# A decode kernel: fewer, larger VectorE instructions per K tile, and w2 in two halves with a cast and a store each

## The chip, the cores and the metric

The kernel runs on one core of one Trainium2 chip. The metric is the device time of one execution in microseconds (us). The kernel before takes 661.6 us, and its own runs lie within 0.7 us of each other in any one set of rounds. The span in a profile is about 1.5 us shorter than the timed run. A load "lands" when the last of its 16 parts, one for each DMA engine, has reported its end. The profile also records the TensorE clock as 1.0 (full) or 0.5 (half).

## The reference, cut to what matters

Four sequences decode one token. An attention block over a cache of 4096 positions and 32 heads is followed by a small dense block. The caches dominate: `k_cache` and `v_cache` are 134 MB each, all weights together 15 MB.

```python
q = (layernorm(x) @ wq)                        # 4 x 640 -> 4 x 32 x 128
scores = einsum("bhqd,bhkd->bhqk", q, k_cache) * Dh ** -0.5
o = einsum("bhqk,bhkd->bhqd", softmax(scores), v_cache)
h = x + o.reshape(B, Sq, H * Dh) @ wo
act = mish(layernorm(h) @ w1 + b1)
out = h + act @ w2                             # w2: 1728 x 640
```

## The kernel before

The caches are cut into 16 K tiles and 16 V tiles of 8.4 MB (8 heads of one sequence each). They pass through three SBUF slots, A, B and C. All loads are issued by one engine, SyncE, in order, into one queue. Tiles come in four groups of four (`b` is 0 to 3). The order of loads and what each waits for:

```python
for hg in range(NHG):                       # i = hg * 4 is the group's first tile
    ...
    sp.need(("F", i + 1, NS - 1)); k_load(i + 3)      # slot B
    sp.need(("F", i + 2, NS - 1)); v_load(i + 2)      # slot A: free when the last fold of K tile i+2 is done
    sp.need(("PV", i + 1));        v_load(i + 3)      # slot C
```

For each K tile, in four slices `s`: VectorE multiplies the slice with q in place (`M`), TensorE adds up columns by 16 matmuls with an identity (`F`, the "fold"), VectorE reduces the rest (`R`), ScalarE takes exp. When the four slices are through, VectorE spreads the exp values over 8 head columns (the mask, `e`) and TensorE multiplies with V (`PV`). The VectorE order of a tile, and TensorE's order for the third and fourth tile of a group:

```python
# VectorE, tile i
mult(i, 0); mult(i, 1); reduce(i, 0); mult(i, 2)
reduce(i, 1); mult(i, 3); reduce(i, 2); reduce(i, 3)
for s in range(NS):
    mask(i, s)
# TensorE
for b in (2, 3):
    fold(i + b, 0); fold(i + b, 1); fold(i + b, 2)
    pv_mm(i + b - 1)
    fold(i + b, 3)
    o_mm(i + b - 1)
```

At the end the weights come through the same queue: wo, w1, and w2 last, in pieces. The 640 output columns are computed as four groups of 160 on four column groups of TensorE, cast by one VectorE instruction, and stored by two DMAs on each of two queues. Four dummy matmuls (`busy(4)`) stand before the w2 matmuls, while TensorE waits for `act`.

The softmax here doesn't subtract the row's maximum and nothing guards it: scores larger than these inputs give would overflow.

Of the kernel before, what the change touches and what calls it, by code (L numbers as in the profile page):

```python
# [7 lines left out]
FP32 = mybir.dt.float32  # L8
# [70 lines left out]
def kernel(  # L79
# [39 lines left out]
    OC = D // CG  # L119
# [39 lines left out]
    rs1 = sb("rs1", (P, N), FP32)  # L159
    rsm = sb("rsm", (P, N, G), FP32)  # L160
    rl = sb("rl", (BG, 1), FP32)
    bmask = sb("bmask", (BG, G), FP32)
    rlm = sb("rlm", (BG, G), FP32)
    hmask_f = sb("hmask_f", (P, G), FP32)
    hmask = sb("hmask", (P, G), BF16)
    delta_f = sb("delta_f", (BG, N), FP32)
# [30 lines left out]
    zeros = sb("zeros", (P, OC), BF16, tail, topA)  # L197
# [3 lines left out]
    mu = sb("mu", (P, N), FP32, tail, topA)  # L201
    esq = sb("esq", (P, N), FP32, tail, topA)
    cen = sb("cen", (P, DC, N), BF16, tail, topA)
    msq = sb("msq", (P, N), FP32, tail, topA)
# [6 lines left out]
    h_hi = sb("h_hi", (P, DC, N), BF16, tail, topA)  # L211
    h_lo = sb("h_lo", (P, DC, N), BF16, tail, topA)
# [27 lines left out]
    y2_ps = red[:, 0, 0:OC]  # L240
# [24 lines left out]
    def store(p, h):  # L265
        p.need("o_bf")
        for k in range(h, CG, 2):
            load(
                p, out_rows[:, k * OC : (k + 1) * OC], o_bf[k * QD : k * QD + N, :],
                ("out", k), f"OUT{h}",  # L270
            )

    def leave(p, h):
        fin, o = book.handles["FIN"], book.handles[f"OUT{h}"]
        if p.live:
            p.eng.sem_inc(fin, 1)
            p.eng.wait_ge(o, 32).then_inc(o, -32)
# [73 lines left out]
    def pool_prog():  # L351
# [13 lines left out]
        po.do(lambda: g.memset(ones[:, :], 1.0), "ones", "PO")  # L365
        po.need(("PV", NT - 2))
        po.do(lambda: g.memset(ones_d[:, :], 1.0 / D), "ones_d", "PO")
        po.do(lambda: g.memset(zeros[:, :], 0.0), "zeros", "PO")

    def act_prog():  # L370
# [21 lines left out]

        ac.need("ident")
# [7 lines left out]
        def exp(i, s):  # L401
# [8 lines left out]
                ("exp", i, s), "AC",  # L410
# [31 lines left out]
        )  # L442
        store(ac, 1)
        leave(ac, 1)

    def dve_prog():
# [5 lines left out]
        for k in range(2):  # L452
# [14 lines left out]
                out=hmask_f[:, :], in_=ident[:, :].rearrange("p (g q) -> p g q", g=G),  # L467
                axis=AX.X, op=ALU.add,
            ),
            "hmask_f", DV,  # L470
# [3 lines left out]
                out=bmask[:, :], in_=ident[0:BG, 0:BG].rearrange("p (b g) -> p g b", g=G),  # L474
                axis=AX.X, op=ALU.add,
            ),
            "bmask", DV,
        )
        dv.do(
            lambda: v.tensor_reduce(  # L480
                out=delta_f[:, :], in_=ident[0:BG, 0:BG].rearrange("p (b g) -> p b g", g=G),
                axis=AX.X, op=ALU.add,
            ),
            "delta_f", DV,
# [10 lines left out]
        dv.need("delta_f")  # L495
        dv.do(lambda: v.tensor_copy(out=hmask[:, :], in_=hmask_f[:, :]), "hmask", DV)
        dv.do(lambda: v.tensor_copy(out=delta[:, :], in_=delta_f[:, :]), "delta", DVP)
# [20 lines left out]
        dv.need("b1p", "b1z")  # L518
        dv.do(lambda: v.tensor_copy(out=b1T[:, 0:FM], in_=b1_ps[:, 0:FM]), "b1m", DV)  # L519
        dv.do(lambda: v.tensor_copy(out=b1T[0:FT, FM:FC], in_=b1_ps[0:FT, FM:FC]), "b1T", DVP)  # L520
        dv.do(lambda: v.memset(rsm[:, :, :], 1.0), ("rsm", -1), DVP)
        dv.need(("qc", N - 1), "hmask")

        def mult(i, s):
            hg, b = divmod(i, N)
            t = slot[KS[b]][:, :].rearrange("p (r d) -> p r d", d=Dh)[:, s * RS : (s + 1) * RS, :]
            dv.need(("K", i))
            dv.do(
                lambda: v.tensor_tensor(  # L529
                    out=t, in0=t, in1=q_bc[:, hg, b, :].unsqueeze(1).to_broadcast([P, RS, Dh]),  # L530
                    op=ALU.mult,
                ),
                ("M", i, s), DVP,
            )
# [13 lines left out]
        def mask(i, s):  # L548
            sl = slice(s * RS, (s + 1) * RS)
            dv.need(("exp", i, s))  # L550
            if i:
# [3 lines left out]
                    out=e[:, sl, :], in0=ex[:, sl].unsqueeze(2).to_broadcast([P, RS, G]),  # L555
                    in1=hmask[:, :].unsqueeze(1).to_broadcast([P, RS, G]), op=ALU.mult,
                ),
                ("e", i, s), DVP,
            )

        def sums(hg):
            dv.do(
                lambda: v.tensor_reduce(
                    out=rs1[:, :], in_=rs[:, :, :], axis=AX.X, op=ALU.add
                ),
                ("rs1", hg), DV,
            )
            dv.need(("rs1", hg))
            dv.do(
                lambda: v.tensor_tensor(  # L570
                    out=rsm[:, :, :], in0=rs1[:, :].unsqueeze(2).to_broadcast([P, N, G]),
                    in1=hmask[:, :].unsqueeze(1).to_broadcast([P, N, G]), op=ALU.mult,
# [4 lines left out]
        def norm(hg):  # L577
            dv.need(("L", hg))
            dv.do(lambda: v.reciprocal(out=rl[:, :], in_=l_ps), ("rl", hg), DV)  # L579
            dv.need(("rl", hg))  # L580
            dv.do(
                lambda: v.tensor_scalar(
                    out=rlm[:, :], in0=bmask[:, :], scalar1=rl[:, :], scalar2=None, op0=ALU.mult
                ),
                ("rlm", hg), DV,
            )
            dv.need(("rlm", hg), ("O", hg * N + N - 1))
            dv.do(
                lambda: v.tensor_tensor(
                    out=om[:, :, :], in0=o_ps.unsqueeze(1).to_broadcast([BG, G, Dh]),  # L590
                    in1=rlm[:, :].unsqueeze(2).to_broadcast([BG, G, Dh]), op=ALU.mult,
# [10 lines left out]
        for i in range(NT):  # L602
            hg, b = divmod(i, N)
            mult(i, 0)
            mult(i, 1)
            reduce(i, 0)
# [430 lines left out]
```

## Time and profile before

Median 661.67 us (661.51 to 661.71, 3 runs). Profiled span 660.0 us.

| what | value | where |
|---|---|---|
| share of 16 DMA engines' span in the load queue | 99.4% | the DMA queues |
| spacing of 8.4 MB tiles at the end of the queue | 19.3 us each | landing records |
| VectorE busy | 62% | the busy table |
| slack of the third V load of each group over the end of the load ahead of it | 9.3, 6.8, 7.7, 9.0 us | issue times and landing records |
| from the last landing to the end | 2.5 us | 660.04 - 657.57 |

The page of the kernel before: its span, the busy times by engine, the DMA rate in 40 equal slices, the load queue (packets, MB, share of 16 engines), and two instruction groups with count, busy time, mean ns of one, and the idle time ahead of them. PE is TensorE, DVE VectorE, ACT ScalarE; SPq is SyncE issuing a DMA, PEq TensorE's instruction sequencer; L529 is line 529 of the kernel.

```profile
span 660.0 us, 4989 instructions
...
PE 383.8 (58%) x2636; PEld 68.4 (10%) x1680; DVE 407.8 (62%) x257; ACT 40.7 (6%) x157; POOL 1.7 (0%) x12
...
GB/s 418 409 445 445 438 441 417 422 441 438 438 437 425 429 437 437 441 437 421 433 437 437 441 437 417 437 437 433 441 441 417 437 433 437 441 441 417 425 416 312
...
q1 hardware_dynamic: 6912, 283.35, 99.4%
...
L529 DVE TENSOR_TENSOR slotA<-slotA,q_bc 128x8192 bf16<-128x8192 bf16 x32 | 140.7, 4416 | 93.1 <-DMA slotA<-in_A_k_cache_dram 93.1
...
L554 DVE TENSOR_TENSOR e<-ex,hmask 128x512 bf16<-128x512 bf16 x64 | 39.8, 684 | 0.0
```

The DMA row never falls below 409 GB/s before the last slice: the kernel runs at the rate of its loads. Work on the engines costs time only where a load is issued too late, or after the last load has landed.

The timeline of the kernel before around the third K tile of the second group (start us, length us, engine, what; in brackets the idle time before it):

```profile
250.67 8.75 DVE L529 TENSOR_TENSOR slotA<-slotA,q_bc 128x8192 bf16<-128x8192 bf16 x2
255.24 0.59 PE L730 MATMUL red<-slotA,ident 128*128 128x512 bf16 x1 [8.15 <-PEq L49]
255.62 5.99 PE L740 MATMUL red<-slotA,ident 128*128 128x512 bf16 x15
261.64 1.23 DVE L540 TENSOR_REDUCE s_f<-red 128x64 f32<-128x1024 f32 x1 [2.21 <-PE red L740]
262.78 4.42 DVE L529 TENSOR_TENSOR slotA<-slotA,q_bc 128x8192 bf16<-128x8192 bf16 x1
...
267.34 0.38 PE L730 MATMUL red<-slotA,ident 128*128 128x512 bf16 x1 [2.29 <-PEq L49]
267.56 5.08 PE L740 MATMUL red<-slotA,ident 128*128 128x512 bf16 x15
...
272.57 3.64 PE L730 MATMUL pv<-slotC,e 128*32 128x512 bf16 x64
...
276.37 3.40 PE L740 MATMUL red<-slotA,ident 128*128 128x512 bf16 x15
...
279.80 0.33 SPq L263 DMA_DIRECT2D slotA<-in_A_v_cache_dram  x1
```

The four folds start at 255.2, 261.4, 267.3 and 276.1. The last one releases the V load at 279.80. The load ahead of it landed at 286.61, so it was issued 6.8 us ahead of need.

The end of the kernel before, from the same view:

```profile
652.03 0.71 PE L730 MATMUL red<-cen,slotB 128*64 128x4 bf16 x14
...
652.78 0.22 DVE L693 TENSOR_TENSOR h<-red,rstd 128x56 f32<-128x56 f32 x1 [2.85 <-PE red L730]
...
654.32 0.22 DVE L719 SCALAR_TENSOR_TENSOR act<-tb,hm 128x56 bf16<-128x56 f32 x1
...
655.13 1.27 PE L730 MATMUL red<-slotA,act 128*4 128x160 bf16 x32
...
657.23 0.62 PE L730 MATMUL red<-slotA,act 128*4 128x160 bf16 x20 [0.83 <-DMA slotA<-in_B_w_dram]
657.91 0.32 DVE L726 CAST o_bf<-red 128x160 bf16<-128x160 f32 x1 [3.37 <-PE red L730]
658.26 0.65 SPq L263 DMA_DIRECT2D out_dram<-o_bf  x2
```

The w2 matmuls wait for w2: the last piece's 16 parts are in at 657.57, and the last matmul ends at 657.85.

### The profile page before, as it was taken

Reading aid. Unit: us, or ns where it says so; the run is one execution under the profiler, and the core shown is the slowest. Engines: PE = TensorE matmul, PEld = TensorE weight load, DVE = VectorE, ACT = ScalarE, POOL = GpSimd, SP = SyncE. Lnnn points to the kernel's source line nnn. Section 1 sums busy time; section 2 is a strip of 40 time slices with the busy share of each in tenths; the row PEclk is TensorE's granted clock in tenths of the full one; section 3 lists DMA queues with packets and bytes.
Section 4 is the critical chain, followed back from the end, with each engine's and each line's share of the span. In section 5 each row is a group of like instructions: output and inputs, shape, how many; then the busy total and the mean of one; then the engine's idle time right before and its main releaser. Section 6 shows DMA issues by size and latency. Waiting matters only on the chain. (4 is left out here: it accounts for less than half of the span.)

```text
span 660.0 us, 4989 instructions
## 1 busy us (share of the span) xinstructions
PE 383.8 (58%) x2636; PEld 68.4 (10%) x1680; DVE 407.8 (62%) x257; ACT 40.7 (6%) x157; POOL 1.7 (0%) x12
## 2 busy tenths in 40 slices
PE   1255758457327595838307395838434757665877
PEld 0000100101101010101100010000110001010145
DVE  1087988386048778677219798749206688957612
ACT  0200000000000000000000000000000000000011
POOL 0000000000000000000000000000000000000000
PEclk9778787879659796869668887879876769796868
DMA  9999999999999999999999999999999999999997
GB/s 418 409 445 445 438 441 417 422 441 438 438 437 425 429 437 437 441 437 421 433 437 437 441 437 417 437 437 433 441 441 417 437 433 437 441 441 417 425 416 312
DMA packets 6954, 283.50 MB, mean 430 GB/s; under 512 B 857, under 2 KB 1184, under 8 KB 2208
## 3 DMA queue, kind: packets, MB, share of 16 engines
q1 hardware_dynamic: 6912, 283.35, 99.4%
q8 instruction: 7, 0.11, 0.1%
q14 instruction: 3, 0.02, 0.0%
q10 hardware_dynamic: 32, 0.01, 0.0%
HBM read 283.35 MB, written 0.01 MB: 429 GB/s over the span
## 5 line engine op out<-in xcount | busy, mean ns | idle before, releaser
L529 DVE TENSOR_TENSOR slotA<-slotA,q_bc 128x8192 bf16<-128x8192 bf16 x32 | 140.7, 4416 | 93.1 <-DMA slotA<-in_A_k_cache_dram 93.1
L529 DVE TENSOR_TENSOR slotB<-slotB,q_bc 128x8192 bf16<-128x8192 bf16 x32 | 140.7, 4418 | 18.4 <-DMA slotB<-in_A_k_cache_dram 18.4
L540 DVE TENSOR_REDUCE s_f<-red 128x64 f32<-128x1024 f32 x64 | 78.0, 1219 | 96.3 <-PE red L740 96.2
L740 PE MATMUL red<-slotA,ident 128*128 128x512 bf16 x480 | 135.8, 446 | 0.0
L740 PE MATMUL red<-slotB,ident 128*128 128x512 bf16 x480 | 126.1, 422 | 0.0
L730 PE MATMUL red<-slotA,ident 128*128 128x512 bf16 x32 | 14.7, 458 | 129.4 <-PEq L49 129.4
L730 PE MATMUL pv<-slotC,e 128*32 128x512 bf16 x768 | 51.9, 430 | 37.3 <-PEq L49 34.3
L730 PE MATMUL red<-slotB,ident 128*128 128x512 bf16 x32 | 14.2, 443 | 89.1 <-PEq L49 89.1
L406 ACT ACTIVATE ex<-s_f 128x64 bf16<-128x64 f32 x64 | 16.4, 256 | 513.3 <-DVE s_f L540 513.3
L554 DVE TENSOR_TENSOR e<-ex,hmask 128x512 bf16<-128x512 bf16 x64 | 39.8, 684 | 0.0
L730 PEld LDWEIGHTS pv<-slotC,e 128*32 128x32 bf16 x768 | 22.1, 106 | 95.4 <-issue 81.3
L730 PEld LDWEIGHTS red<-slotA,ident 128*128 128x128 bf16 x32 | 3.2, 99 | 198.0 <-issue 197.9
L730 PEld LDWEIGHTS red<-slotB,ident 128*128 128x128 bf16 x32 | 3.1, 98 | 171.1 <-issue 171.1
L730 PEld LDWEIGHTS o_ps<-pv_sb,selo 128*32 128x32 f32 x136 | 13.5, 109 | 62.6 <-issue 62.6
L730 PE MATMUL o_ps<-pv_sb,selo 128*32 128x128 f32 x136 | 18.0, 276 | 0.0
L730 PE MATMUL pv<-slotA,e 128*32 128x512 bf16 x256 | 14.5, 380 | 0.6 <-PEq L49 0.5
L416 ACT COPY pv_sb<-pv 128x512 f32<-128x512 f32 x16 | 9.4, 586 | 69.5 <-PE pv L730 69.5
L406 ACT ACTIVATION_READ_ACCUMULATOR ex<-s_f 128x1 f32 x64 | 11.9, 186 | 0.0
L730 PEld LDWEIGHTS pv<-slotA,e 128*32 128x32 bf16 x256 | 6.9, 97 | 23.6 <-issue 17.8
L579 DVE RECIPROCAL rl<-misc 32x1 f32<-32x1 f32 x4 | 0.6, 150 | 12.6 <-PE misc L730 12.6
L519 DVE CAST b1T<-pv 128x13 bf16<-128x13 f32 x1 | 0.2, 174 | 12.1 <-PE pv L730 12.1
L730 PE MATMUL y_ps<-a_t,slotB 128*128 128x64 bf16 x160 | 7.3, 211 | 0.0
(107 smaller groups left out, 69.2 us busy)
## 6 DMA issues: line engine op xcount, KB each, us to landing
slotC<-in_A_v_cache_dram SPq DMA_DIRECT2D x2, 4096.0 KB, 42.2
slotC<-in_A_wq_dram SPq DMA_DIRECT2D x1, 5120.0 KB, 15.4
slotB<-in_A_wo_dram SPq DMA_DIRECT2D x3, 1280.0 KB, 15.4
slotA<-in_B_w_dram SPq DMA_DIRECT2D x3, 640.0 KB, 13.9
slotB<-in_B_w_dram SPq DMA_DIRECT2D x2, 864.0 KB, 22.1
slotB<-in_A_wo_dram SPq DMA_DIRECT2D x1, 640.0 KB, 19.0
slotB<-in_A_wo_dram SPq DMA_DIRECT2D x1, 480.0 KB, 19.8
slotB<-in_B_w_dram SPq DMA_DIRECT2D x1, 432.0 KB, 22.8
```

The lines of the kernel that those rows point to most:

```text
L406: lambda: a.activation(out=ex[:, sl], in_=s_f[:, sl], func=ACT.Exp, scale=SCALE, accum_out=rs[:, b, s : s + 1],),
L416: lambda: a.copy(out=pv_sb[:, :, :].rearrange("p r d -> p (r d)"), in_=pv[:, :]),
L519: dv.do(lambda: v.tensor_copy(out=b1T[:, 0:FM], in_=b1_ps[:, 0:FM]), "b1m", DV)
L529: lambda: v.tensor_tensor(out=t, in0=t, in1=q_bc[:, hg, b, :].unsqueeze(1).to_broadcast([P, RS, Dh]), op=ALU.mult,),
L540: lambda: v.tensor_reduce(out=s_f[:, s * RS : (s + 1) * RS], in_=red[:, k : k + 2, :].rearrange("p k (r c) -> p (k r) c", c=CW), axis=AX.X ...
L554: lambda: v.tensor_tensor(out=e[:, sl, :], in0=ex[:, sl].unsqueeze(2).to_broadcast([P, RS, G]), in1=hmask[:, :].unsqueeze(1).to_broadcast( ...
L579: dv.do(lambda: v.reciprocal(out=rl[:, :], in_=l_ps), ("rl", hg), DV)
L730: lambda: nc.tensor.matmul(out_, lhsT=lhsT, rhs=rhs, start=start, stop=stop, skip_group_check=skip),
L740: return t.add_instruction(mybir.InstMatmult(name=nc.get_next_instruction_name(), engine=mybir.EngineType.PE, ins=[t.lower_ap(rhs), t.lowe ...
```

## The change

Its intent is a shorter VectorE program, and an end with less work in series. Per K tile it has two products over two slices each in place of four, and one mask in place of four. The sum and norm steps of a group are fused; two small setup copies go to ScalarE. w2 runs as two halves of 320 columns, cast on two engines, each with one store. The dummy matmuls before w2 go, and the residual is added by fp32 matmuls instead of a high and a low bf16 part. The diff, cut to its core (the many renamed tiles, the setup and the norm are left out):

```diff
 # VectorE, per tile
-        t = slot[KS[b]]...[:, s * RS : (s + 1) * RS, :]
+        t = slot[KS[b]]...[:, s * RS : (s + 2) * RS, :]
             mult(i, 0)
-            mult(i, 1)
-            reduce(i, 0)
             mult(i, 2)
...
+            reduce(i, 0)
             reduce(i, 1)
-            mult(i, 3)
             reduce(i, 2)
...
             reduce(i, 3)
-            for s in range(NS):
-                mask(i, s)
+            mask(i)
 # TensorE, fold
-        pe.need(("M", i, s))
+        pe.need(("M", i, s // 2 * 2))
+        if s > 1:
+            pe.need(("exp", i, s - 2))
 # the end
-        busy(4)
         pe.need("act")
-            for k in range(CG):                       # 4 groups of 160 columns
+            for k in range(KO):                       # 2 groups of 320 columns
...
-        dv.need("y2")
-        dv.do(lambda: v.tensor_copy(out=o_bf[:, :], in_=y2_ps), "o_bf", DV)
+        dv.need(("y2", 0))
+        dv.do(lambda: v.tensor_copy(out=o_bf[0:N, :], in_=y2_ps[0:N, 0, :]), ("o_bf", 0), DV)
+        # and on ScalarE: need ("y2", 1), copy to o_bf[QD : QD + N, :], store
```

More of the change, by code (lines that the diff above doesn't have):

```diff
@@ L118 @@
     BG = N * G
-    OC = D // CG
+    KO = 2
+    OC = D // KO
     QN = G * Dh
@@ L158 @@
     rs = sb("rs", (P, N, NS), FP32)
-    rs1 = sb("rs1", (P, N), FP32)
-    rsm = sb("rsm", (P, N, G), FP32)
+    rsm = sb("rsm", (P, NS, N, G), FP32)
     rl = sb("rl", (BG, 1), FP32)
     bmask = sb("bmask", (BG, G), FP32)
-    rlm = sb("rlm", (BG, G), FP32)
-    hmask_f = sb("hmask_f", (P, G), FP32)
     hmask = sb("hmask", (P, G), BF16)
-    delta_f = sb("delta_f", (BG, N), FP32)
     delta = sb("delta", (BG, N), BF16)
@@ L196 @@
     ones_d = sb("ones_d", (P, P), FP32, tail, topA)
-    zeros = sb("zeros", (P, OC), BF16, tail, topA)
+    zeros = sb("zeros", (P, 1), BF16, tail, topA)
+    ident_f = sb("ident_f", (P, P), FP32, tail, topA)
     ysum = sb("ysum", (P, N), FP32, tail, topA)
@@ L200 @@
     sq = sb("sq", (P, DC, N), FP32, tail, topA)
-    mu = sb("mu", (P, N), FP32, tail, topA)
     esq = sb("esq", (P, N), FP32, tail, topA)
     cen = sb("cen", (P, DC, N), BF16, tail, topA)
+    mu = sb("mu", (P, N), FP32, tail, topA)
     msq = sb("msq", (P, N), FP32, tail, topA)
@@ L210 @@
     b1_lo = sb("b1_lo", (P, FC, N), BF16, tail, topA)
-    h_hi = sb("h_hi", (P, DC, N), BF16, tail, topA)
-    h_lo = sb("h_lo", (P, DC, N), BF16, tail, topA)
     act = sb("act", (P, FC, N), BF16, tail, topA)
@@ L239 @@
     h1_ps = h1_w[:, 0:FC, 0, :]
-    y2_ps = red[:, 0, 0:OC]
+    y2_ps = red[:, 0:KO, 0:OC]
     x_rows = A_x.rearrange("b s d -> (b s) d")
@@ L265, in store @@
     def store(p, h):
-        p.need("o_bf")
-        for k in range(h, CG, 2):
-            load(
-                p, out_rows[:, k * OC : (k + 1) * OC], o_bf[k * QD : k * QD + N, :],
-                ("out", k), f"OUT{h}",
-            )
+        p.need(("o_bf", h))
+        load(
+            p, out_rows[:, h * OC : (h + 1) * OC], o_bf[h * QD : h * QD + N, :],
+            ("out", h), f"OUT{h}",
+        )
     def leave(p, h):
@@ L276, in leave @@
             p.eng.sem_inc(fin, 1)
-            p.eng.wait_ge(o, 32).then_inc(o, -32)
+            p.eng.wait_ge(o, 16).then_inc(o, -16)
     def clear():
@@ L365, in pool_prog @@
         po.do(lambda: g.memset(ones[:, :], 1.0), "ones", "PO")
+        po.do(lambda: g.memset(rsm[:, :, :, :], 1.0), "rsmz", "PO")
         po.need(("PV", NT - 2))
@@ L368, in pool_prog @@
         po.do(lambda: g.memset(zeros[:, :], 0.0), "zeros", "PO")
+        po.do(lambda: g.tensor_copy(out=ident_f[:, :], in_=ident[:, :]), "ident_f", "PO")
     def act_prog():
@@ L391, in act_prog @@
             )
+        ac.need("b1p", "b1z")
+        ac.do(lambda: a.copy(out=b1T[:, 0:FM], in_=b1_ps[:, 0:FM]), "b1m", "AC")
+        ac.do(lambda: a.copy(out=b1T[0:FT, FM:FC], in_=b1_ps[0:FT, FM:FC]), "b1T", "ACP")
         ac.need("ident")
@@ L409, in exp @@
                 ),
-                ("exp", i, s), "AC",
+                ("exp", i, s), "ACP" if s < NS // 2 else "AC",
             )
@@ L442, in act_prog @@
         )
+        ac.need(("y2", 1))
+        ac.do(
+            lambda: a.copy(out=o_bf[QD : QD + N, :], in_=y2_ps[QD : QD + N, 1, :]), ("o_bf", 1), "AC"
+        )
         store(ac, 1)
@@ L466, in dve_prog @@
             lambda: v.tensor_reduce(
-                out=hmask_f[:, :], in_=ident[:, :].rearrange("p (g q) -> p g q", g=G),
-                axis=AX.X, op=ALU.add,
+                out=hmask[:, :], in_=ident[:, :].rearrange("p (g q) -> p g q", g=G),
+                axis=AX.X, op=ALU.max,
             ),
-            "hmask_f", DV,
+            "hmask", DV,
         )
@@ L473, in dve_prog @@
             lambda: v.tensor_reduce(
-                out=bmask[:, :], in_=ident[0:BG, 0:BG].rearrange("p (b g) -> p g b", g=G),
-                axis=AX.X, op=ALU.add,
-            ),
-            "bmask", DV,
-        )
-        dv.do(
-            lambda: v.tensor_reduce(
-                out=delta_f[:, :], in_=ident[0:BG, 0:BG].rearrange("p (b g) -> p b g", g=G),
-                axis=AX.X, op=ALU.add,
-            ),
-            "delta_f", DV,
+                out=delta[:, :], in_=ident[0:BG, 0:BG].rearrange("p (b g) -> p b g", g=G),
+                axis=AX.X, op=ALU.max,
+            ),
+            "delta", DVP,
         )
@@ L494, in dve_prog @@
         )
-        dv.need("delta_f")
-        dv.do(lambda: v.tensor_copy(out=hmask[:, :], in_=hmask_f[:, :]), "hmask", DV)
-        dv.do(lambda: v.tensor_copy(out=delta[:, :], in_=delta_f[:, :]), "delta", DVP)
+        dv.need("sel_f")
         dv.do(
@@ L517, in dve_prog @@
         dv.do(lambda: v.tensor_copy(out=xT[:, :, :], in_=tpx[:, :, :]), "xT", DVP)
-        dv.need("b1p", "b1z")
-        dv.do(lambda: v.tensor_copy(out=b1T[:, 0:FM], in_=b1_ps[:, 0:FM]), "b1m", DV)
-        dv.do(lambda: v.tensor_copy(out=b1T[0:FT, FM:FC], in_=b1_ps[0:FT, FM:FC]), "b1T", DVP)
-        dv.do(lambda: v.memset(rsm[:, :, :], 1.0), ("rsm", -1), DVP)
+        dv.do(
+            lambda: v.tensor_reduce(
+                out=bmask[:, :], in_=ident[0:BG, 0:BG].rearrange("p (b g) -> p g b", g=G),
+                axis=AX.X, op=ALU.add,
+            ),
+            ("rsm", -1), DVP,
+        )
         dv.need(("qc", N - 1), "hmask")
@@ L525, in mult @@
             hg, b = divmod(i, N)
-            t = slot[KS[b]][:, :].rearrange("p (r d) -> p r d", d=Dh)[:, s * RS : (s + 1) * RS, :]
+            t = slot[KS[b]][:, :].rearrange("p (r d) -> p r d", d=Dh)[:, s * RS : (s + 2) * RS, :]
             dv.need(("K", i))
@@ L529, in mult @@
                 lambda: v.tensor_tensor(
-                    out=t, in0=t, in1=q_bc[:, hg, b, :].unsqueeze(1).to_broadcast([P, RS, Dh]),
+                    out=t, in0=t, in1=q_bc[:, hg, b, :].unsqueeze(1).to_broadcast([P, 2 * RS, Dh]),
                     op=ALU.mult,
@@ L546, in reduce, with mask @@
             )
-        def mask(i, s):
-            sl = slice(s * RS, (s + 1) * RS)
-            dv.need(("exp", i, s))
+        def mask(i):
+            dv.need(("exp", i, NS - 1))
             if i:
@@ L554, in mask @@
                 lambda: v.tensor_tensor(
-                    out=e[:, sl, :], in0=ex[:, sl].unsqueeze(2).to_broadcast([P, RS, G]),
-                    in1=hmask[:, :].unsqueeze(1).to_broadcast([P, RS, G]), op=ALU.mult,
+                    out=e[:, :, :], in0=ex[:, :].unsqueeze(2).to_broadcast([P, R, G]),
+                    in1=hmask[:, :].unsqueeze(1).to_broadcast([P, R, G]), op=ALU.mult,
                 ),
-                ("e", i, s), DVP,
+                ("e", i), DVP,
             )
@@ L562, in sums @@
             dv.do(
-                lambda: v.tensor_reduce(
-                    out=rs1[:, :], in_=rs[:, :, :], axis=AX.X, op=ALU.add
-                ),
-                ("rs1", hg), DV,
-            )
-            dv.need(("rs1", hg))
-            dv.do(
                 lambda: v.tensor_tensor(
-                    out=rsm[:, :, :], in0=rs1[:, :].unsqueeze(2).to_broadcast([P, N, G]),
-                    in1=hmask[:, :].unsqueeze(1).to_broadcast([P, N, G]), op=ALU.mult,
+                    out=rsm[:, :, :, :],
+                    in0=rs[:, :, :].rearrange("p b s -> p s b").unsqueeze(3).to_broadcast([P, NS, N, G]),
+                    in1=hmask[:, :].unsqueeze(1).unsqueeze(1).to_broadcast([P, NS, N, G]), op=ALU.mult,
                 ),
@@ L579, in norm @@
             dv.do(lambda: v.reciprocal(out=rl[:, :], in_=l_ps), ("rl", hg), DV)
-            dv.need(("rl", hg))
+            dv.need(("rl", hg), ("O", hg * N + N - 1))
             dv.do(
-                lambda: v.tensor_scalar(
-                    out=rlm[:, :], in0=bmask[:, :], scalar1=rl[:, :], scalar2=None, op0=ALU.mult
-                ),
-                ("rlm", hg), DV,
-            )
-            dv.need(("rlm", hg), ("O", hg * N + N - 1))
-            dv.do(
-                lambda: v.tensor_tensor(
-                    out=om[:, :, :], in0=o_ps.unsqueeze(1).to_broadcast([BG, G, Dh]),
-                    in1=rlm[:, :].unsqueeze(2).to_broadcast([BG, G, Dh]), op=ALU.mult,
+                lambda: v.scalar_tensor_tensor(
+                    out=om[:, :, :], in0=bmask[:, :].unsqueeze(2).to_broadcast([BG, G, Dh]),
+                    scalar=rl[:, 0:1], in1=o_ps.unsqueeze(1).to_broadcast([BG, G, Dh]),
+                    op0=ALU.mult, op1=ALU.mult,
                 ),
@@ L664, in dve_prog @@
         )
-        dv.do(lambda: v.tensor_copy(out=h_hi[:, :, :], in_=st[:, :, :]), "h_hi", DV)
         dv.need("std2")
@@ L676, in dve_prog @@
         dv.do(lambda: v.reciprocal(out=rstd[:, :], in_=std2[:, :]), "rstd", DV)
-        dv.need("h_hi")
-        dv.do(
-            lambda: v.tensor_tensor(
-                out=h_lo[:, :, :], in0=st[:, :, :], in1=h_hi[:, :, :], op=ALU.subtract
-            ),
-            "h_lo", DV,
-        )
         dv.need("b1_hi")
@@ L734, in mm, with mm_same @@
         )
-    def mm_same(out_, lhsT, rhs, start, stop, mark=None):
+    def mm_same(out_, lhsT, rhs, start, stop, mark=None, skip=True):
         t = nc.tensor
@@ L746, in emit @@
                     tile_size=(P, P), tile_position=(0, 0), ldweights=False,
+                    bass_skip_group_check=skip,
                 )
@@ L808, in fold @@
                 )
-                mm(*args, skip=False) if first else mm_same(*args)
+                (mm if first else mm_same)(*args, skip=False)
     def pv_mm(i):
         t = slot[VS[i % N]][:, :]
-        pe.need(("e", i, NS - 1), ("V", i))
+        pe.need(("e", i), ("V", i))
         nu = R // RQ
@@ L836, in l_mm @@
         pe.need(("rsm", hg))
-        mm(l_ps, rsm[:, :, :].rearrange("p b g -> p (b g)"), ones[:, :], True, True, ("L", hg))
+        for s in range(NS):
+            mm(
+                l_ps, rsm[:, s, :, :].rearrange("p b g -> p (b g)"), ones[:, :],
+                s == 0, s == NS - 1, ("L", hg) if s == NS - 1 else None,
+            )
     def a_mm(hg):
@@ L886, in busy @@
         def busy(n):
-            for _ in range(n):
-                mm(o_full[:, :], ident[:, :], zeros[:, 0:1].to_broadcast([P, 512]), True, True)
+            for k in range(n):
+                (mm_same if k else mm)(
+                    o_full[:, :], ident[:, :], zeros[:, :].to_broadcast([P, 512]), True, True
+                )
         hg = NHG - 1
@@ L896, in pe_tail @@
         a_mm(hg)
-        pe.need("zeros", ("e", NT - 1, NS - 1))
-        for k in (2, 3):
-            mm(red[:, k, :], ident[:, :], zeros[:, 0:1].to_broadcast([P, 512]), True, False)
-        mm(y2_ps, ident[:, :], zeros[:, 0:OC], True, False)
+        pe.need("zeros", ("e", NT - 1))
+        for k, w in enumerate((OC, OC, 512, 512)):
+            (mm_same if k else mm)(
+                red[:, k, 0:w], ident[:, :], zeros[:, :].to_broadcast([P, w]), True, False
+            )
         wo_mm(2)
@@ L912, in pe_tail @@
                 pe.need("b1_lo")
-                for part in (b1_hi, b1_lo):
+                for n, part in enumerate((b1_hi, b1_lo)):
                     for j0, j1 in ((0, FC // 2 + 1), (FC // 2 + 1, FC)):
-                        mm(h1_ps[:, j0:j1, :], ident[:, :], part[:, j0:j1, :], False, False)
+                        (mm_same if n or j0 else mm)(
+                            h1_ps[:, j0:j1, :], ident[:, :], part[:, j0:j1, :], False, False
+                        )
             pe.need(("w1", c0))
@@ L931, in pe_tail @@
                     )
-        pe.need("h_lo", "h_hi")
-        for part in (h_hi, h_lo):
-            for k in range(CG):
-                for c in range(DC):
-                    mm(
-                        y2_ps[k * QD : k * QD + N, :].rearrange("b (m c) -> b c m", c=DC)[:, c, :],
-                        part[:, c, :], ident[:, k * QD : (k + 1) * QD], False, False,
-                    )
-        busy(4)
+        pe.need("st", "ident_f")
+        for c in range(DC):
+            for k in range(KO):
+                mm(
+                    y2_ps[k * QD : k * QD + N, k, :].rearrange("b (m c) -> b c m", c=DC)[:, c, :],
+                    st[:, c, :], ident_f[:, k * P // KO : (k + 1) * P // KO], False, False,
+                )
         pe.need("act")
@@ L944, in w2_mm @@
             rows = P if j < FM else FT
-            for k in range(CG):
+            for k in range(KO):
                 cs = slice(k * OC, (k + 1) * OC)
-                done = j == FM - 1 and k == CG - 1
                 mm(
-                    y2_ps[k * QD : k * QD + N, :], act[0:rows, j, :],
+                    y2_ps[k * QD : k * QD + N, k, :], act[0:rows, j, :],
                     w2_sb[:, j, cs] if j < FM else w2_tail[0:FT, cs], False, j == FM - 1,
-                    "y2" if done else None,
+                    ("y2", k) if j == FM - 1 else None,
                 )
@@ L963, in pe_prog @@
         pe_setup()
-        pe.need("selo", "xT", "b1T")
+        pe.need("selo", "xT", "b1T", "rsmz")
         logs = []
```

## The prediction

> **What bounds the kernel.** The DMA engines. The DMA-queue view gives the load queue 99.4% of 16 engines' span; 283.5 MB go through at about 430 GB/s. The tile (slot) views and the landing records show 8.4 MB tiles landing every 19.3 us from start to end, without a gap until 656.3 of 660.0 us. VectorE (62% busy) and TensorE (58%) only decide when slots come free, so their time counts only (a) where a load is issued so late that the queue runs dry, and (b) after the last w2 piece lands (657.57 us) until the end: 2.4 us.
>
> **What the change saves off the path.** Per K tile VectorE has 4 products (4.42 us each), 4 reductions (1.22), 4 masks (2.49 together): about 25 us. Two double products and one mask save about 0.4 us per tile; the fused norm saves a 0.2 us step. Worth nothing directly.
>
> **What it moves.** Before, reduction 0 follows product 1, so reductions and folds overlap products. After, both double products (about 17.4 us) come first; fold 2 waits for exp 0, hence for reduction 0 at about 18.7 us. I worked the order through with the trace's durations (fold 3.45 us at full clock, 5 to 6.4 after idling; PV 3.6; exp 0.45). The last fold of a tile ends some 3 us later than before, the masked probabilities likewise; over three consecutive tiles this adds up to 8 or 9 us. The tight load is V of the third tile in each head group, which needs that last fold. The queue's timeline shows it issued at 122.8, 279.8, 433.5, 586.7 us, when the preceding load landed at 132.1, 286.6, 441.2, 595.7: slack 9.3, 6.8, 7.7, 9.0 us. Afterwards I expect 0 to 2 us. An issued load's first packets start about 1.0 us later (first load in the trace), so four bubbles of 0 to 2 us each: total +2.5 us (estimate; 0 to 9). Other loads keep 3 us or more.
>
> The clock makes this uncertain. The Trainium skill ("TensorE: Matmul & The Clock Gate", Part 1) says that the clock halves after an idle window of about 3.4 us and needs a busy one to recover. The trace agrees: clock records of 1.0 and 0.5 in multiples of 3.41 us, folds of 6.4 and 3.6 us. The shorter wait between folds 1 and 2 (1.5 instead of 2.3 us) should keep fold 2 warm.
>
> **Tail.** w2 as two 320-column groups instead of four 160-column ones halves the packing: the last 20 small matmuls took 0.62 us; 10 larger ones need 0.7 warm, 1.3 at half clock: +0.1 to +0.7. Casts of 4x320 on two engines instead of one 0.32 us: +0.1. One store per queue instead of two in series (second store's packets began 0.33 us after the first's): -0.33. Net about +0.3 us.
>
> **Prediction.** 664.5 us, range 661.2 to 671. Faster by over 2%: 0.01; within 2%: 0.93; slower by over 2%: 0.06.
>
> **What would show it.** VectorE busy down about 15 us; queue share still near 99%; the third V of each group issued 6 to 9 us later relative to the preceding landing; landings still 19.3 us apart except for up to four gaps of 20 to 21.5; final packets of each store in one group.
>
> **What would make it wrong.** If folds run colder, fold 2 costs 1.7 us more and each bubble reaches 3 to 5 us, giving 675 or more. If slack stays above 1 us everywhere, the time is 661.5 to 662. If the double product does not keep its rate (over 9 us), bubbles grow.

## The result, and the profile after

Median 670.02 us (669.40 to 671.49, 4 runs) against 661.59 us (4 runs). The ratio is 1.0131, 95% interval 1.0116 to 1.0146. Here and below a ratio is the mean time of one kernel's runs over that of the other's of the same rounds, so not quite the ratio of the medians that are quoted. So the changed kernel is 8.4 us slower. That is inside the predicted range, but the forecast was +2.9 us: the size is wrong.

The page of the changed kernel, the same lines:

```profile
span 668.0 us, 4849 instructions
...
PE 377.0 (56%) x2619; PEld 70.2 (11%) x1651; DVE 402.6 (60%) x162; ACT 41.3 (6%) x160; POOL 1.9 (0%) x14
...
GB/s 436 420 409 432 440 440 440 378 440 441 437 428 436 440 420 432 432 385 424 440 440 440 440 440 440 440 377 440 440 436 420 400 440 440 440 440 440 408 409 267
...
q1 hardware_dynamic: 6904, 283.35, 98.7%
...
L527 DVE TENSOR_TENSOR slotA<-slotA,q_bc 128x16384 bf16<-128x16384 bf16 x16 | 138.3, 8686 | 95.0 <-DMA slotA<-in_A_k_cache_dram 95.0
...
L551 DVE TENSOR_TENSOR e<-ex,hmask 128x2048 bf16<-128x2048 bf16 x16 | 36.7, 2292 | 6.6 <-ACT ex L406 6.6
```

VectorE has 95 instructions fewer and 5.2 us less work. Yet the DMA row now has three slices of 377 to 385 GB/s: the 8th, 18th and 27th, at about 117 to 134, 284 to 301 and 434 to 451 us. These are the places where the third V load of the first three groups begins.

The timeline of the changed kernel at the same K tile (the third of the second group):

```profile
257.09 17.28 DVE L527 TENSOR_TENSOR slotA<-slotA,q_bc 128x16384 bf16<-128x16384 bf16 x2
265.92 0.59 PE L704 MATMUL red<-slotA,ident 128*128 128x512 bf16 x1 [12.71 <-PEq L49]
266.30 5.69 PE L714 MATMUL red<-slotA,ident 128*128 128x512 bf16 x15
...
272.04 3.40 PE L714 MATMUL red<-slotA,ident 128*128 128x512 bf16 x15
274.29 2.41 DVE L538 TENSOR_REDUCE s_f<-red 128x64 f32<-128x1024 f32 x2
...
276.04 0.38 PE L704 MATMUL red<-slotA,ident 128*128 128x512 bf16 x1 [0.59 <-PEq L49]
276.25 3.40 PE L714 MATMUL red<-slotA,ident 128*128 128x512 bf16 x15
...
279.58 3.64 PE L704 MATMUL pv<-slotC,e 128*32 128x512 bf16 x64
...
283.38 3.40 PE L714 MATMUL red<-slotA,ident 128*128 128x512 bf16 x15
...
286.81 0.33 SPq L259 DMA_DIRECT2D slotA<-in_A_v_cache_dram  x1
```

Now both products run first (17.28 us), the first reduction starts only behind them, and fold 2 waits for the exp of slice 0. The K tile landed at 249.30, but its first product starts at 257.09, 7.8 us later; before it was 2.7 us (247.98 and 250.67). The two tiles ahead of it ended late. The V load is issued at 286.81, and the load ahead of it landed at 287.92: 1.1 us of lead, where there were 6.8.

The end of the changed kernel:

```profile
659.46 0.73 PE L704 MATMUL red<-cen,slotB 128*64 128x4 bf16 x14
...
660.23 0.22 DVE L667 TENSOR_TENSOR h<-red,rstd 128x56 f32<-128x56 f32 x1 [3.51 <-PE red L704]
...
661.77 0.22 DVE L693 SCALAR_TENSOR_TENSOR act<-tb,hm 128x56 bf16<-128x56 f32 x1
...
662.40 3.63 PE L704 MATMUL red<-slotA,act 128*4 128x320 bf16 x26
666.06 0.48 DVE L700 CAST o_bf<-red 4x320 bf16<-4x320 f32 x1 [4.07 <-PE red L704]
666.10 0.42 ACT L445 CAST o_bf<-red 4x320 bf16<-4x320 f32 x1 [5.37 <-PE red L704]
666.57 0.30 SPq L259 DMA_DIRECT2D out_dram<-o_bf  x1
```

The last landing is at 663.40, so here the w2 matmuls do not wait for w2: they fill TensorE from 662.04 to 666.03, at half clock (the clock records show 0.5 from 653.2 to the end).

The landing records split the difference of the two profiles (7.9 us):

| stretch | before | after | difference |
|---|---|---|---|
| start to landing of the last V tile | 634.34 | 639.51 | +5.17 |
| to the landing of the last w2 piece | 23.23 | 23.89 | +0.66 |
| to the end | 2.47 | 4.56 | +2.09 |

So there are two things to explain: a DMA queue that runs dry in the loop, and a longer end. (The middle stretch was not followed up. In the second profile of the changed kernel, g3, it is 22.65 us, so its +0.66 is no fixed cost.)

**Theory.** The third V load of a group is issued too late because the reductions now stand behind the products. A load needs a certain lead over the end of the load ahead of it; the prediction put this at 1.0 us, and it is larger. **Rivals.** The changed instructions themselves slow the DMA or the engines (the double product, the single mask); or the end of the kernel costs it all.

A measure used below, "queue loss", is worked out from the packet records. Around the start of each load I sum the time in which a DMA engine had no packet, and what first packets took above 2.418 us (the usual time of a 64 KiB packet), over all engines, divided by 16. The kernel before has 0.0 us, the changed one 5.25 us. The measure reaches only 2.5 us beyond a landing, so it is short where a gap is longer than that, and it can miss part of a loss: the last V tile of e3 and g3 came 10.4 and 7.75 us later than in the kernel before, their queue losses are 8.3 and 6.2.

### The profile page after: what moved, and what is told of

The parts are those of the page before. It is cut to its first block, busy times and chain, and to the rows that moved or that the text cites. A ratio compares the mean times of both kernels' runs of the same rounds, so it can differ in the third digit from the quotient of the medians.

```text
span 668.0 us, 4849 instructions
## 1 busy us (share of the span) xinstructions
PE 377.0 (56%) x2619; PEld 70.2 (11%) x1651; DVE 402.6 (60%) x162; ACT 41.3 (6%) x160; POOL 1.9 (0%) x14
## 5 line engine op out<-in xcount | busy, mean ns | idle before, releaser
L527 DVE TENSOR_TENSOR slotA<-slotA,q_bc 128x16384 bf16<-128x16384 bf16 x16 | 138.3, 8686 | 95.0 <-DMA slotA<-in_A_k_cache_dram 95.0
L527 DVE TENSOR_TENSOR slotB<-slotB,q_bc 128x16384 bf16<-128x16384 bf16 x16 | 138.3, 8684 | 0.0
L714 PE MATMUL red<-slotA,ident 128*128 128x512 bf16 x480 | 126.6, 423 | 0.0
L704 PE MATMUL red<-slotA,ident 128*128 128x512 bf16 x32 | 13.9, 434 | 145.4 <-PEq L49 145.4
L551 DVE TENSOR_TENSOR e<-ex,hmask 128x2048 bf16<-128x2048 bf16 x16 | 36.7, 2292 | 6.6 <-ACT ex L406 6.6
L704 PEld LDWEIGHTS y_ps<-a_t,slotB 128*128 128x128 bf16 x160 | 6.9, 131 | 3.9 <-issue 3.0
L704 PE MATMUL red<-slotC,lnT 128*32 128x512 bf16 x40 | 3.8, 556 | 5.7 <-PEq L49 5.7
```

Source lines behind the costliest of these rows:

```text
L527: lambda: v.tensor_tensor(out=t, in0=t, in1=q_bc[:, hg, b, :].unsqueeze(1).to_broadcast([P, 2 * RS, Dh]), op=ALU.mult,),
L551: lambda: v.tensor_tensor(out=e[:, :, :], in0=ex[:, :].unsqueeze(2).to_broadcast([P, R, G]), in1=hmask[:, :].unsqueeze(1).to_broadcast([P, ...
L704: lambda: nc.tensor.matmul(out_, lhsT=lhsT, rhs=rhs, start=start, stop=stop, skip_group_check=skip),
L714: return t.add_instruction(mybir.InstMatmult(name=nc.get_next_instruction_name(), engine=mybir.EngineType.PE, ins=[t.lower_ap(rhs), t.lowe ...
```

## The experiments

Times are medians; "before" was run in the same rounds each time (661.77, 661.42 and 661.52 us).

### e1: the loop put back in the changed kernel

```diff
 # the changed kernel, per-tile program of the kernel before
+            mult(i, 0); mult(i, 1); reduce(i, 0); mult(i, 2)
+            reduce(i, 1); mult(i, 3); reduce(i, 2); reduce(i, 3)
+            for s in range(NS): mask(i, s)
-            mult(i, 0); mult(i, 2); reduce(i, 0); ... ; mask(i)     # double products
-        if s > 1: pe.need(("exp", i, s - 2))
```

> The changed kernel with only the per-tile VectorE program put back (four products with the reductions between them, four masks, fold 2 not waiting for an exp); setup, sums, norm and the whole tail stay changed. Loop theory (the third V load of a group is issued too late and the queue runs dry, 4.4 to 5.2 of the 8.4 us): no landing gap over 20.2 us after the start, slack of the third V about 7 to 9 us, total 662.5 to 665. If the loop were innocent and the tail cost everything: still about 670. Tail theory: from the last w2 landing to the end stays near 4 us where the clock is at half, against 2.5 before.

Measured 662.06 us (662.01 to 662.11, 4 runs), ratio 1.0005. Queue loss 0.1 us. The page line of its load queue:

```profile
q1 hardware_dynamic: 6904, 283.35, 99.3%
```

With the loop put back nearly all of the 8.4 us is gone. The rest of the change, the end included, costs about 0.3 us, less than the interval of the ratio (0.9988 to 1.0022) resolves. The total lies a little below the range that I expected, and two leads of the third V loads, 5.8 and 6.7 us, below the 7 to 9. From the last landing to the end this profile has 3.09 us, not the 4 us that I expected.

### e2: the changed loop alone, in the kernel before

```diff
 # the kernel before, with the change's per-tile program (products, reductions, mask, exp wait) and nothing else
-            mult(i, 0); mult(i, 1); reduce(i, 0); ...
+            mult(i, 0); mult(i, 2); reduce(i, 0); ...; mask(i)
```

> The kernel before with only the per-tile VectorE program changed (two double products first, one mask, fold 2 behind exp 0). Loop theory: three or four landing gaps of 20 to 21.5 us after the third V load's issue, total 666 to 668, with the last 2.5 us as before. If the parts add up, this excess and that of the loop-undone kernel sum to 8.4 us. Rival (the tail causes all): 661.6.

Measured 673.97 us (670.79 to 674.78, 4 runs), ratio 1.0173. Queue loss 11.4 us; from the last landing to the end 2.49 us, as before. The loop alone is enough: the loss does not need the changed end. But it cost 12 us, more than I expected and more than the whole change: the parts do not add up. Its runs spread over 4 us. Whether the change's other parts (the shorter norm) really save some 4 us in the loop, or whether this is chance (see g3), these runs do not settle.

### e3: the four dummy matmuls put back before w2

```diff
+        busy(4)
         pe.need("act")
```

> The changed kernel with the four dummy matmuls before the w2 matmuls put back. Theory that their removal leaves the clock at half for the w2 matmuls (3.97 us in the changed kernel): clock full during most of w2, w2 matmuls done within about 1 us of the last landing, total about 668.5, 1 to 1.5 us less than 670.0. Rival (the clock fell earlier, at 653 us, from waits for wo, and the dummies come too late or delay w2): total 670 or a little more.

Measured 670.46 us (670.09 to 672.69, 4 runs), ratio 1.0130: no gain in the total. The profile (of the 672.69 us run) explains why that total is no verdict. Its end was shorter by 1.5 us, 3.09 us from the last landing, with the clock at full from 667.9. But its queue loss was 8.3 us, where the first profile of the changed kernel has 5.25. The timeline line of its w2 matmuls:

```profile
666.92 2.39 PE L704 MATMUL red<-slotA,act 128*4 128x320 bf16 x26
```

The same 26 matmuls took 3.63 us at half clock. So the half of the theory that speaks of the clock holds. The other profiles agree: in the changed kernel (both profiles), e1, e4 and f1, all without the dummies, the clock record is at 0.5 for nearly all of the w2 matmuls; in all with the dummies it is at 1.0 for at least a third of that stretch. That the dummies save time is not shown. e1 and e4 also end 3.09 us after the last landing, without the dummies: their `act` was ready 2.9 and 3.9 us before that landing, against 1.4 us in the first profile of the changed kernel. The slow matmuls cost most only where `act` is late. The fairest pair is e3 and the second profile of the changed kernel (g3, no dummies): `act` was ready 2.3 us before the last landing in both, and they ended 3.09 and 3.26 us after it: 0.2 us between two single profiles.

### e4: the last fold ahead of the PV matmuls

```diff
             fold(i + b, 2)
-            pv_mm(i + b - 1)
             fold(i + b, 3)
+            pv_mm(i + b - 1)
```

> The changed kernel with one move on TensorE: for the third and fourth tile of a group the last fold goes ahead of the previous tile's PV matmuls. It releases the third V load about 3.6 us sooner. Theory that a load needs a lead of about 2.5 us over the end of the load before it: slack of that load rises from 0.6 to 2.5 us to 4 to 6 us, no landing gap over 20.2 us, total 664 to 665.5. Rival (the lower DMA rate comes from something else, such as the double products' SBUF traffic): gaps stay, total about 670.

Measured 663.62 us (662.97 to 665.16, 4 runs), ratio 1.0026. The timeline of this kernel at the same tile:

```profile
278.64 3.40 PE L714 MATMUL red<-slotA,ident 128*128 128x512 bf16 x15
...
281.97 3.64 PE L704 MATMUL pv<-slotC,e 128*32 128x512 bf16 x64
282.07 0.33 SPq L259 DMA_DIRECT2D slotA<-in_A_v_cache_dram  x1
```

The V load is issued at 282.07 instead of 286.81. No third V load has a gap any more. Queue loss 1.5 us, from small losses at the second V loads of two groups, whose leads were 3.6 and 3.75 us. The landing gaps there were 20.4 and 20.5 us, so my bound of 20.2 was missed; the total is slightly below my range. This run takes nothing away from VectorE and has the same instructions. Only when the slot comes free has moved. That is the strongest evidence for the theory: 6.4 us come back from the order of two groups of matmuls.

### f1: four single products in a row

```diff
-            mult(i, 0)           # double
-            mult(i, 2)           # double
+            mult(i, 0); mult(i, 1); mult(i, 2); mult(i, 3)      # single
```

> The changed kernel with the two double products of a tile split into four single ones, still all before the first reduction; mask, exp wait and tail stay changed. Theory 'order' (reduction 0 waits for the last product, so fold 2, the last fold and the third V load are late): third V loads are issued as in the changed kernel, within 1 us, queue loss 4 to 11 us, total 667 to 674. Rival 'length' (the double product itself, because fold 0 starts 4.4 us later): third V loads issued about 4 us sooner, loss under 2 us, total 662 to 665.

Measured 677.46 us (677.28 to 677.62, 4 runs), ratio 1.0241: slower than the change. The third V loads were issued at 132.1, 292.5, 450.1 and 607.2 us, 2.5 to 9 us later than in the changed kernel (delays of earlier groups included; their leads are 1.1 to 3.3 us shorter), so "within 1 us" failed, and the total lies above my range. But the direction is plain: it is the order, not the length of the product. (No run separates the order of the products from fold 2's wait for exp 0, which goes with it.) The timeline at the same tile shows what I had left out:

```profile
278.92 0.59 PE L706 MATMUL red<-slotA,ident 128*128 128x512 bf16 x1 [5.88 <-PEq L49]
279.30 6.07 PE L716 MATMUL red<-slotA,ident 128*128 128x512 bf16 x15
...
292.52 0.33 SPq L259 DMA_DIRECT2D slotA<-in_A_v_cache_dram  x1
```

With single products, folds 0 and 1 run early. TensorE then idles 5.88 us until the exp of slice 0, its clock halves, and fold 2 takes 6.45 us instead of 3.6. In 12 of the 16 tiles of this profile fold 2 takes 4.9 us or more; in the changed kernel it takes 3.6 to 3.8 in all 16. So the double product helps here: it starts the folds late enough that they run on into fold 2 at full clock.

### f2: the single mask alone, in the kernel before

```diff
-            for s in range(NS):
-                mask(i, s)
+            mask(i)
```

> The kernel before with only the four masks of a tile joined into one. Theory 'order': the mask comes after the last fold of its tile, and joined it ends within 0.3 us of where the four ended; slack of the third V loads stays 6 to 10 us, no queue loss, total 661.5 to 662. Rival (the joined mask's wait for the last exp is part of the loss): some landing gaps above 20.2 us, total over 663.

Measured 661.66 us (661.53 and 661.80), ratio 1.0003. Queue loss 0.0. So the single mask alone costs no time. It may still take a part in the delay: the leads of the third V loads are 8.2, 5.7, 6.6 and 7.6 us, 1.1 to 1.4 us shorter than in the kernel before (one is below the 6 to 10 that I expected), where the whole change takes 5.7 to 7.1 us. Whether that is the mask or the variation between profiles is not shown: e1, with four masks, has 10.8, 8.5, 5.8 and 6.7.

### f3 and f4: a dose of delay in the kernel before

```diff
-            reduce(i, 3)
+            for again in range(n, -1, -1):        # n = 2 in f3, 4 in f4; same result
+                reduce(i, 3, again)
+                dv.need(("R", i, 3, again) if again else ("F", i, 3))
```

> Dose: the kernel before with the last reduction of each tile done three times instead of once (same result), about 2.5 us more VectorE time per tile and 5 us less lead for each third V load: leads over the last landing of 4, 2, 2.5 and 4 us. Lead theory (a load must be issued some 2 to 3.5 us before the load ahead of it ends, or engines idle and the first packets run slow): small losses at the two tightest loads, total 662 to 665. Rival (what costs is the changed instructions themselves, not late loads): 661.6.

> Dose: the same with the last reduction done five times, about 5 us more per tile and 10 us less lead: leads of about -1, -3, -2.5 and -1 us. Lead theory: losses at every third V load of 3 to 6 us, total 673 to 685. Rival (late loads do not matter): 661.6.

Measured: f3 664.79 us (664.60 and 664.98), ratio 1.0050; f4 687.06 us (686.25 and 687.88), ratio 1.0387, a little above my range. All products, folds and masks are those of the kernel before. Lateness alone produces the loss. It is also steep: the first 2.5 us per tile cost 3.4 us in total, the next 2.5 us another 22. Of f4's 25 us about 20 are in the loop (its last V tile landed at 654.18, against 634.34) and 4 at the end, where `act` was ready only 3.2 us after the last landing. f4's timeline at the second group, where the load ahead had landed at 289.66:

```profile
292.19 0.33 SPq L263 DMA_DIRECT2D slotA<-in_A_v_cache_dram  x1
```

These runs together give a dose curve; the table has a selection of their loads. "Lead" is the time from the issue of a third V load to the last landing of the load ahead of it; "gap" is how much later than 19.3 us after that it landed:

| run and load | lead (us) | gap (us) |
|---|---|---|
| before, group 2 | 6.8 | 0.0 |
| f3, group 2 | 3.8 | 0.8 |
| changed, group 4 | 2.5 | 0.1 |
| changed, group 1 | 2.3 | 1.1 |
| changed, group 2 | 1.1 | 1.4 |
| changed, group 3 | 0.6 | 1.9 |
| f1, group 4 | 0.3 | 2.1 |
| f1, group 3 | -0.5 | 3.0 |
| f1, group 2 | -2.2 | 4.7 |
| f4, group 2 | -2.5 | 5.1 |

In most rows the gap is about 2.5 us minus the lead, with small losses up to a lead of 4 us. The prediction took 1.0 minus the lead. Other loads lie well above this line, three of e2's by 2.1 to 2.7 us. The last landing tells only a part: in e2 the 16 engines ended the load ahead 1.9 to 2.9 us apart, so the first of them idled long before the last one was done. Where lead and gap are both taken from the mean of a load's 16 landings, they come together: for all 27 cache loads with such a mean lead under 2.25 us, in all profiles and e2's included, lead and gap add up to 2.1 to 2.8 us.

The packet records of the changed kernel show what this is made of, at the third group's load. It was issued at 443.23. The first engine starts its first packet at 444.18, the last at 444.92. These first packets take 2.7 to 3.3 us instead of 2.42. And a landing is recorded some 0.3 us after the last data packet of its engine has ended, so an engine is idle earlier than the landing says.

f4's timeline has one more line of use: there all of w2 is in before `act` is ready, and its matmuls are those of the kernel before, at full clock.

```profile
681.59 1.07 PE L732 MATMUL red<-slotA,act 128*4 128x160 bf16 x52
```

The same work took 3.63 us as 26 matmuls of 320 columns at half clock, and 2.39 us in e3, where the clock became full on the way. The trace's start times give the step for one row block of w2: four matmuls of 160 columns 69 ns at full clock and 133 at half; two of 320 columns 136 and 267.

### g2: the changed loop with the last fold first, and the old end

```diff
 # e2 with e4's move
             fold(i + b, 2)
+            fold(i + b, 3)
             pv_mm(i + b - 1)
-            fold(i + b, 3)
```

> The kernel before with the changed per-tile VectorE program (as in the run of the loop alone, 674.0 us) and with the last fold ahead of the PV matmuls for the third and fourth tile. Lead theory: the third V loads are issued about 3.6 us sooner, the losses at them go, only small ones at the second V loads stay (about 1.5 us); with the tail of before, total 662.5 to 664.5. Rival (something else in the changed loop costs): over 668.

Measured 663.33 us (661.49 to 664.24, 4 runs), ratio 1.0017 (interval 0.9998 to 1.0035); queue loss 0.8 us. The 12 us of e2 are nearly gone, by the same move of one fold. The leads of its third V loads are 6.7, 5.4, 5.5 and 4.3 us, where e2 has 2.7, 2.1, 1.6 and 1.8. Its issue at the second group, 5.6 us sooner than in e2 (287.41):

```profile
281.84 0.33 SPq L263 DMA_DIRECT2D slotA<-in_A_v_cache_dram  x1
```

It confirms the cause on the other base.

### g3: the changed kernel a second time

No edit.

> The changed kernel, unchanged, for a second profile. Theory that the loss depends on how the windows of the TensorE clock fall on the folds: total between 668 and 673 again, but the queue loss (5.2 us in the first profile) and the end after the last landing (4.6 us) each differ by 0.5 us or more from the first profile, with the same instructions. Rival (a fixed loss): both within 0.3 us of the first profile.

Measured 669.77 us (669.47 and 670.08), ratio 1.0123. The span is 668.0 us, as in the first profile, but made up otherwise. The last V tile landed at 642.09 (+7.75 us over the kernel before, queue loss 6.2 us), and from the last w2 landing to the end it took 3.26 us instead of 4.56. The clock was at full until 662.1 here, and at half from 653.2 in the first profile; `act` was ready 2.3 us before the last landing instead of 1.4. So the loss is not fixed: it varies between profiles of one program, and the records show the clock halving at different places. That the clock is what makes the loss vary is not shown.

No experiment pointed to a version faster than the kernel before. The loads fill the queue there without a gap, and what is left at the end is 2.5 us. The best variants with the shorter VectorE program come within 2 us of it.

## Why the prediction was right or wrong

The path was right (the third V load of a group comes late and the queue runs dry) and the sizes were wrong. The prediction's sum was +2.5 us for the loop and +0.3 us for the end; the profile has +5.2 us for the loop, +0.7 us to the last landing and +2.1 us for the end. The step that failed most is the 1.0 us of lead that a load was taken to need.

- **"The DMA engines bound it; VectorE time counts only where the queue runs dry or after the last landing."** Right. 5.2 us less VectorE work gained nothing, and f2 with the single mask alone took the same time.
- **"The tight load is the third V of each group."** Right: three of its four loads show a gap in the changed kernel (1.1, 1.4, 1.9 us), and releasing it sooner removes the loss (e4, g2).
- **"Afterwards I expect 0 to 2 us" of slack.** Nearly right: 2.3, 1.1, 0.6 and 2.5 us, and the loads were 5.7 to 7.1 us later relative to the landing ahead (6 to 9 forecast).
- **"An issued load's first packets start about 1.0 us later, so four bubbles of 0 to 2 us each: total +2.5 us."** This step failed, in size. The first packet does start after 0.95 us, but the 16 engines start up to 0.75 us apart and their first packets are some 0.3 to 0.9 us longer. A load needed about 2.5 us of lead, and some lost up to 1.2 us at leads of up to 4.1. With the leads that came about, 1.0 minus the lead makes 0.4 us over the four loads; their gaps were 4.5 us. That the forecast had 2.5 us is luck: a need of 1.0 us and slacks of 0 to 2 us make bubbles of 0 to 1 us, not the 0 to 2 that it names. The last V tile came 5.2 us late in the first profile and 7.75 us in the second, where I had +2.5.
- **"Other loads keep 3 us or more."** True, but 3 us is not safe: in e3 and e4 second V loads with leads of 3.6 to 4.1 us lost a little.
- **"The shorter wait between folds 1 and 2 should keep fold 2 warm."** Right: fold 2 takes 3.6 to 3.8 us in all 16 tiles of the changed kernel's first profile, and f1 shows the opposite case (6.45 us). The Trainium skill ("TensorE: Matmul & The Clock Gate", Part 1) led there.
- **"Net about +0.3 us" for the end.** Near where the loop did not disturb it: e1 costs 0.3 us in time, 0.6 us in its profile. In the changed kernel the end cost +2.1 us in one profile and +0.8 us in the other. The terms for packing (twice the time per row block) and for the stores (one group of packets) were right. What I missed is that at half clock the w2 matmuls need 4.0 us in all and become the limit, because `act` was ready only 1.4 us before the last landing (3.0 us in the kernel before). Taking away the dummy matmuls goes with the half clock in w2 (e3), but at equal lateness of `act` the ends with and without them differ by only 0.2 us (e3 against g3). Why the clock fell already at 653.2 in one profile and at 662.1 in the other was not tested and stays open.
- **"VectorE busy down about 15 us."** Wrong: 5.2 us. My own 0.4 us per tile over 16 tiles makes 6.4; the 15 did not follow from it.

## What to carry to other kernels

When a kernel runs at the rate of its loads, count for each load how long before the end of the load ahead it is issued. A rearrangement that shortens a busy engine's program can still cost time if it delays the step that frees a buffer; here moving one group of matmuls ahead of another undid the harm. Do not spend that lead down to the latency of the first packet: here, of twelve loads with 3.4 to 4.1 us of it, seven still landed 0.8 to 1.2 us late and five did not, and between 4.2 and 7 us none lost more than 0.2. And a repeat of the same program can differ by 1 or 2 us in where it loses time.

## What the Trainium skill lacked or had wrong

- "DMA: Bandwidth & Descriptors" (Specifications) gives a first-byte latency of about 0.6 us for loads issued from SyncE. Here the first packet came 0.95 us after the start of the issue, and the last of 16 engines started after 1.7 us. I found no figure there for what it takes to refill a queue that has run dry, which is what counted here: about 2.5 us of lead, with first packets of 2.7 to 3.3 us instead of 2.42.
- The same table has an HBM limit of about 358 GB/s for one core. The page itself says further down ("Measured") that this is the share with both cores of a pair loading. This kernel, a program on one core, read from HBM at 429 GB/s over its whole span of 660 us, near the page's fabric ceiling of 435 GB/s: read alone, the row would have misled.
- "TensorE: Matmul & The Clock Gate" (HAM oscillation) warns of idle gaps over about 3.4 us. Here a shorter pause could be enough: before fold 2 of eight tiles of the kernel before TensorE pauses for 2.29 us, and in five of them fold 2 then takes 5.2 to 5.3 us, in three 3.6 us. In the tile shown (265.06 to 267.34) the clock record goes to 0.5 at 267.67, at the end of a 3.41 us stretch in which TensorE had worked for about a third of the time.
- "TensorEngine Tiling (Array Packing)" (Theoretical Speedup) promises up to four times for a small dimension of at most 32. The traces agree as far as they go: for outputs of 4 rows, four groups of 160 columns take 69 ns per row block, two groups of 320 take 136. No run here has an unpacked w2, so the factor of four itself is not tested.
